# Accumulator banks of their own for each MLP stage, attention steps skewed over three chunks, and a reordered start, in a fused retention and MLP kernel

## The chip, the cores and the metric

The kernel runs on one core of one Trainium2 chip. The metric is the device time of one execution in microseconds (us). The kernel before and the changed one were measured in the same rounds. Two levels occur, about 2 us apart in the kernel before, and where a difference is that small, runs of the same granted TensorE clock (the share of its full rate that TensorE was given, as a mean over the run) are compared.

## The reference

Eight batches of eight heads, 576 positions, head size 64. The scores of q and k are scaled by 1/8 and multiplied by a decay that is lower triangular, `gamma_h ** (i - j)`; there is no softmax. The result (4608 tokens by 512) goes through an MLP with the activation `h * cos(h)`.

```python
scores = scale * np.matmul(q, k.transpose(0, 1, 3, 2))
ret = scores * np.where(rel >= 0, gamma ** rel, 0.0)
attn = np.matmul(ret, v)                      # then (b, h, s, d) -> x[b*s, h*d]
h = x @ w_in                                  # 4608 x 512 @ 512 x 2048
out = (h * np.cos(h)) @ w_out                 # 2048 -> 512
```

## The kernel before

Attention works on chunks of at most 128 positions of one batch (five per batch, the last of 64; 40 in all). The decay is split into a factor in k's position, folded into v by GpSimd (`wv`), and one in q's position, applied at the end (`up`), so earlier chunks enter through a 64 by 64 state per head (`st`). A chunk passes through these steps:

- cast of q, k, v to bf16 (`nat`);
- T: eight transposes into the bank `tp`, one copy by ScalarE to `qk`;
- S: score matmuls into `sc`, masked by VectorE into `pt`;
- ST: the state into `st`, masked by VectorE into `sbd`;
- O: the outputs into `tp` again, scaled by VectorE into `xt`.

The MLP works on blocks of 512 tokens. A first-stage unit is four matmuls of 512 columns into a bank `ml`; ScalarE takes the sine of it shifted by a quarter turn (`cb`), VectorE multiplies (`gt`). A second-stage tile is 16 matmuls of 512 columns in four units; ScalarE evicts it (`os`) and it is stored. The program divides PSUM, the memory that matmuls write to, into eight banks of 512 columns: one `tp`, two `sc`, one `st`, and four `ml`, over which both stages rotate together.

Each engine takes its instructions in the order in which the program adds them (in the profile of this kernel ScalarE's copy for chunk 0, whose transposes end at 7.9 us, starts at 16.66, behind the cast of chunk 3's q, which waits for its load until 16.12); a helper adds the semaphore waits that the named buffers require.

```python
def bank(self):                       # both MLP stages
    i = self.n_ml % 4
    self.n_ml += 1
    return i, self.ML[i]
...
def mlp1(self, j, f):
    i, ps = self.bank()               # four matmuls, sine, product
...
def mlp2(self, j, t, qd):
    if qd == 0:
        self.m2 = self.bank()         # one bank for four units
...
def steps(g):
    def prep():
        cast_to(g + 3)
        load_to(g + 3 + self.NSTG - 1)
        self.step_t(g)
    yield prep
    yield lambda: self.step_s(g)
    if CHUNKS[g][1] < 4:
        yield lambda: self.step_st(g)
    yield lambda: self.step_o(g)

load_to(4)
cast_to(4, ("act", "dve", "pool"))    # q on ScalarE, k on VectorE, v on GpSimd
for s in range(4):
    self.load_win(s)                  # 512 KB slabs of weights, GpSimd's queue
for s in range(4):
    self.load_wout(s)
load_to(self.NSTG)
done = need[0]
for g in range(done):                 # chunks 0 to 3, one after another
    for st in steps(g):
        st()
for j in range(-1, NTB):              # then, for each block: first stage of j+1,
    ...                               # second stage of j, and the steps of the
                                      # chunks of j+2 spread between the units
```

Of the kernel before, what the change touches and what calls it, by code (L numbers as in the profile page):

```python
# [101 lines left out]
class Kernel:  # L102
# [78 lines left out]
    def load_chunk(self, g):  # L181
        b, r, n = CHUNKS[g]
        slot = g % self.NSTG
        for i in (1, 0, 2):
            self.P.add("sp", lambda e, i=i: e.dma_start(  # L185
                ap(self.STG[slot], 3 * DM, 0, n, i * DM, [D, H], [1, D]),
                bass.AP(self.src[i], (b * H * S + CH * r) * D, [[D, n], [S * D, H], [1, D]])),
                w=[("stg", slot, i)], sem=f"i{slot}_{i}")

    def load_win(self, s):  # L190
        self.P.add("pool", lambda e: e.dma_start(
            ap(self.WIN, 4 * DFF, 0, 128, s * 512, [DFF, 4], [1, 512]),
            bass.AP(self.w_in, s * 512, [[DFF, 128], [128 * DFF, 4], [1, 512]])),
            w=[("win", s)], sem=f"wi{s}")

    def load_wout(self, s):
        self.P.add("pool", lambda e: e.dma_start(
            ap(self.WOUT, NF * DM, 0, 128, s * 4 * DM, [DM, 4], [1, DM]),
            bass.AP(self.w_out, s * 4 * 128 * DM, [[DM, 128], [128 * DM, 4], [1, DM]])),
            w=[("wout", s)], sem=f"wo{s}")  # L200
# [19 lines left out]
    def step_t(self, g):  # L220
        b, r, n = CHUNKS[g]
        na, qk = self.NAT[g % self.NNAT], self.QK[g % self.NQK]
        tb = self.T.ap().bitcast(BF16)

        def mm(e, i):
            for c in range(4):
                inst = e.transpose(  # L227
                    tb[:, (1 - i) * 512 + c * 128:(1 - i) * 512 + c * 128 + n],
                    ap(na, 3 * DM, 0, n, i * DM + 128 * c, [1, 128]),
                    ap(self.IDN, 128, 0, n, 0, [1, n]))  # L230
            return inst

        for i in (1, 0):
            self.P.add("pe", lambda e, i=i: mm(e, i), r=[("nat", g % self.NNAT, i), "idn"], w=["tp"])
        w = [("qk", g % self.NQK)]
        self.P.add("act", lambda e: e.activation(  # L236
            ap(qk, 1024, 0, 128, 0, [128, 8], [1, n]),
            tb.rearrange("p (c n) -> p c n", c=8)[:, :, 0:n], AF.Copy), r=["tp"], w=w)

    def step_s(self, g):  # L240
        b, r, n = CHUNKS[g]
        qk, pt = self.QK[g % self.NQK], self.PT[g % self.NPT]

        def mm(e):
            for c in range(4):
                for hp in range(2):
                    inst = e.matmul(  # L247
                        ap(self.SC, 1024, 0, n, hp * 512 + c * 128, [1, n]),
                        ap(qk, 1024, 64 * hp, 64, c * 128, [1, n]),
                        ap(qk, 1024, 64 * hp, 64, 512 + c * 128, [1, n]),  # L250
                        start=True, stop=True, skip_group_check=True)
            return inst

        self.P.add("pe", mm, r=[("qk", g % self.NQK)], w=["sc"])
        self.P.add("dve", lambda e: e.tensor_tensor(  # L255
            ap(pt, 1024, 0, n, 0, [128, 8], [1, n]),
            ap(self.SC, 1024, 0, n, 0, [128, 8], [1, n]),
            ap(self.TRI, 128, 0, n, 0, [0, 8], [1, n]), ALU.mult),
            r=["sc", "tri"], w=[("pt", g % self.NPT)])
# [22 lines left out]
    def step_o(self, g):  # L282
        b, r, n = CHUNKS[g]
        na, qk, pt = self.NAT[g % self.NNAT], self.QK[g % self.NQK], self.PT[g % self.NPT]
        sbd = self.SBD[(g - 1) % self.NSB]

        def inter(e):
            for c in range(4):
                inst = e.matmul(  # L289
                    ap(self.T, 512, 0, 128, c * 128, [1, n]),  # L290
                    ap(sbd, 512, 0, 128, c * 128, [1, 128]),
                    ap(qk, 1024, 0, 128, 512 + c * 128, [1, n]),
                    start=(c == 0), stop=True, skip_group_check=True)
            return inst

        def intra(e):
            for c in range(4):
                for hp in range(2):
                    inst = e.matmul(  # L299
                        ap(self.T, 512, 64 * hp, 64, c * 128, [1, n]),  # L300
                        ap(na, 3 * DM, 0, n, 2 * DM + (2 * c + hp) * D, [1, D]),
                        ap(pt, 1024, 0, n, hp * 512 + c * 128, [1, n]),
                        start=(r == 0 and c == 0), stop=True, skip_group_check=True)
            return inst

        if r:
            self.P.add("pe", inter, r=[("sbd", (g - 1) % self.NSB), ("qk", g % self.NQK)], w=["tp"])
        self.P.add("pe", intra, r=[("nat", g % self.NNAT, 2), ("pt", g % self.NPT)], w=["tp"])
        self.P.add("dve", lambda e: e.tensor_tensor(  # L309
            ap(self.XT, 4 * TOK, 0, 128, b * S + CH * r, [TOK, 4], [1, n]),  # L310
            ap(self.T, 512, 0, 128, 0, [128, 4], [1, n]),
            ap(self.UP, 4 * S, 0, 128, CH * r, [S, 4], [1, n]), ALU.mult),
            r=["tp", "up"], w=[("xt", g)])


    def bank(self):
        i = self.n_ml % 4
        self.n_ml += 1
        return i, self.ML[i]

    def mlp1(self, j, f):
        i, ps = self.bank()
# [3 lines left out]
        xts = [("xt", g) for g, (b, r, n) in enumerate(CHUNKS)  # L326
               if b * S + CH * r < TB * (j + 1) and b * S + CH * r + n > TB * j]

        def mm(e):
            for c in range(4):  # L330
                inst = e.matmul(  # L331
                    ps.ap(), ap(self.WIN, 4 * DFF, 0, 128, c * DFF + 128 * f, [1, 128]),
                    ap(self.XT, 4 * TOK, 0, 128, c * TOK + TB * j, [1, TB]),
# [4 lines left out]
        self.P.add("act", lambda e: e.activation(cb.ap(), ps.ap(), AF.Sin, bias=self.CPI.ap(), scale=1.0),  # L338
                   r=[("ml", i), "cpi"], w=[("cb", ci)])
        self.P.add("dve", lambda e: e.tensor_tensor(  # L340
            ap(gt, NF * TB, 0, 128, f * TB, [1, TB]), ps.ap(), cb.ap(), ALU.mult),
            r=[("ml", i), ("cb", ci)], w=[("gt", j % 2, f)])

    def mlp2(self, j, t, qd):
        if qd == 0:
            self.m2 = self.bank()
        i, ps = self.m2
        gt = self.GT[j % 2]

        def mm(e, f):  # L350
            return e.matmul(  # L351
                ps.ap(), ap(gt, NF * TB, 0, 128, f * TB + 128 * t, [1, 128]),
                ap(self.WOUT, NF * DM, 0, 128, f * DM, [1, DM]),
                start=(f == 0), stop=(f == NF - 1))

        for f in range(4 * qd, 4 * qd + 4):
            self.P.add("pe", lambda e, f=f: mm(e, f), r=[("gt", j % 2, f), ("wout", f // 4)], w=[("ml", i)])
        if qd == 3:
            o = self.n_os % self.NOS
            self.n_os += 1  # L360
            self.P.add("act", lambda e: e.activation(self.OS[o].ap(), ps.ap(), AF.Copy),  # L361
                       r=[("ml", i)], w=[("os", o)])
            self.P.add("sp", lambda e: e.dma_start(
                bass.AP(self.out, (TB * j + 128 * t) * DM, [[DM, 128], [1, DM]]), self.OS[o].ap()),
                r=[("os", o)], sem=f"o{o}")


    def schedule(self):
        need = []
        for j in range(NTB):  # L370
            need.append(1 + max(g for g, (b, r, n) in enumerate(CHUNKS) if b * S + CH * r < TB * (j + 1)))
        state = {"loaded": 0, "cast": 0}

        def load_to(g):
            while state["loaded"] < min(g, len(CHUNKS)):
                self.load_chunk(state["loaded"])
                state["loaded"] += 1

        def cast_to(g, engs=("pool", "pool", "pool")):
            while state["cast"] < min(g, len(CHUNKS)):  # L380
# [3 lines left out]
        def steps(g):  # L384
            def prep():
                cast_to(g + 3)
                load_to(g + 3 + self.NSTG - 1)
                self.step_t(g)
            yield prep
            yield lambda: self.step_s(g)  # L390
            if CHUNKS[g][1] < 4:
                yield lambda: self.step_st(g)
            yield lambda: self.step_o(g)

        load_to(4)
        cast_to(4, ("act", "dve", "pool"))
        for s in range(4):
            self.load_win(s)
        for s in range(4):
            self.load_wout(s)  # L400
        load_to(self.NSTG)
        done = need[0]
        for g in range(done):
            for st in steps(g):
                st()
        for j in range(-1, NTB):
            todo = []
            if j + 2 < NTB:
                for g in range(done, need[j + 2]):
                    todo += list(steps(g))  # L410
                done = need[j + 2]
            n, k = len(todo), 0
            for i in range(16):
                if j + 1 < NTB:
                    self.mlp1(j + 1, i)
                while k < n * (2 * i + 1) / 32:
                    todo[k]()
                    k += 1
                if j >= 0:
                    self.mlp2(j, i // 4, i % 4)  # L420
                while k < n * (2 * i + 2) / 32:
                    todo[k]()
                    k += 1
# [38 lines left out]
```

## Time and profile before

| kernel before | |
|---|---|
| time, median | 390.75 us (390.64 to 392.42, 4 runs) |
| span of the profiled run | 389.2 us |
| TensorE busy | 84% |
| VectorE, ScalarE busy | 48%, 42% |
| first MLP matmul recorded | 38.0 us |
| part with block 1's second stage begins | 110.3 us |
| last block (second stage only) begins | 372.3 us |

A row of the timeline shows the start, the duration, the engine, the source line, the operation with what it writes and reads, the shape, the number of instructions, and in brackets the idle time before it and what ended that. The first extract is TensorE in the kernel before: two chunks of the head, and one tile end of the part without attention. L227 is T, L247 is S, L267 is ST, L289 and L299 are O, L331 the first stage, L351 the second.

```profile
17.72 0.61 PE L247 MATMUL sc<-qk 64*128 64x128 bf16 x8 [9.80 <-ACT qk L236]
18.26 0.61 PE L267 MATMUL st<-nat 128*128 128x128 bf16 x4
19.65 0.64 PE L299 MATMUL tp<-pt,nat 128*64 128x128 bf16 x8 [0.78 <-DVE pt L255]
21.08 1.03 PE L227 MATMUL tp<-idn,nat 128*128 128x128 bf16 x8 [0.79 <-DVE xt L309]
23.23 0.61 PE L247 MATMUL sc<-qk 64*128 64x128 bf16 x8 [1.12 <-ACT qk L236]
...
38.02 1.48 PE L331 MATMUL ml<-xt,win 128*128 128x512 bf16 x3 [1.20 <-DVE xt L309]
...
346.37 1.03 PE L331 MATMUL ml<-xt,win 128*128 128x512 bf16 x4
347.23 1.03 PE L351 MATMUL ml<-wout,gt 128*128 128x512 bf16 x4
348.95 1.04 PE L331 MATMUL ml<-xt,win 128*128 128x512 bf16 x4 [0.69 <-ACT os L361]
```

In the head, one score group follows the other after 5.5 us (17.72, 23.23), and TensorE is busy for about half of that (2.8 us). At 347.23 the last unit of a tile starts. Units follow each other every 0.86 us, so the next could start at 348.09; it starts at 348.95. The duration of a matmul is modelled to its end in the pipe (379 ns for 512 columns), while the next can start 216 ns after it; so every idle time on TensorE is shown about 0.16 us too short.

The second extract is the view of waits of TensorE (in total, number, longest):

```profile
PE sc L247 <- ACT qk L236: 16.7, 14, 9.8
PE ml L331 <- ACT os L361: 15.3, 25, 0.9
PE tp L227 <- DVE xt L309: 6.5, 7, 2.0
```

The first and third belong mostly to the start (14.8 and 5.9 us of them lie before 72 us). The second is spread over the whole kernel: a first-stage unit takes the bank that a finished tile has just left and waits for ScalarE's eviction.

### The profile page before, as it was taken

Reading aid. Unit: us, or ns where it says so; the run is one execution under the profiler, and the core shown is the slowest. Engines: PE = TensorE matmul, PEld = TensorE weight load, DVE = VectorE, ACT = ScalarE, POOL = GpSimd, SP = SyncE. Lnnn points to the kernel's source line nnn. Section 1 sums busy time; section 2 is a strip of 40 time slices with the busy share of each in tenths; the row PEclk is TensorE's granted clock in tenths of the full one; section 3 lists DMA queues with packets and bytes.
Section 4 is the critical chain, followed back from the end, with each engine's and each line's share of the span. In section 5 each row is a group of like instructions: output and inputs, shape, how many; then the busy total and the mean of one; then the engine's idle time right before and its main releaser. Section 6 shows DMA issues by size and latency. Waiting matters only on the chain.

```text
span 389.2 us, 5828 instructions
## 1 busy us (share of the span) xinstructions
PE 326.4 (84%) x2325; PEld 160.0 (41%) x2368; DVE 185.4 (48%) x283; ACT 162.3 (42%) x231; POOL 91.3 (23%) x128
## 2 busy tenths in 40 slices
PE   1156877889988999989889999998999899989996
PEld 0033433344444444444444444444444444434442
DVE  2245466645554555545554655455555555433310
ACT  6222445344443544445435444444444444444421
POOL 2390147522223222312222222321331000000000
PEclk9999989999999999999999999999999999999999
DMA  9999999995448254552675245442000000010012
GB/s 177 201 201 196 196 214 215 204 216 129 108 116 183 69 109 108 115 103 69 142 155 109 69 108 109 108 109 67 31 27 29 27 29 29 27 48 33 29 54 81
DMA packets 121946, 42.31 MB, mean 109 GB/s; under 512 B 113216, under 2 KB 117312, under 8 KB 121920
## 3 DMA queue, kind: packets, MB, share of 16 engines
q1 hardware_dynamic: 117696, 37.76, 45.9%
q0 software_dynamic: 4224, 4.19, 6.3%
q8 instruction: 18, 0.29, 0.3%
q14 instruction: 8, 0.07, 0.1%
HBM read 36.70 MB, written 9.44 MB: 119 GB/s over the span
## 4 chain that ended last, share of the span: by engine, by line
PE 73%; ACT 12%; DVE 7%; issue 3%; SPq 3%; DMA 1%; DVEq 0%; ACTq 0%
PE ml L331 31%; PE ml L351 30%; ACT qk L236 5%; ACT os L361 4%; PE tp L227 4%; PE sc L247 3%; ACT cb L338 3%; DVE gt L340 3%; PE tp L299 3%; SPq L185 3%; DVE pt L255 2%; DVE xt L309 2%; PE st L267 1%; DMA stg<-in_q_dram 1%; PE tp L289 1%
## 5 line engine op out<-in xcount | busy, mean ns | idle before, releaser
L340 DVE TENSOR_TENSOR gt<-ml,cb 128x512 bf16<-128x512 f32 x144 | 99.5, 691 | 160.3 <-ACT cb L338 142.1
L338 ACT ACTIVATE cb<-ml,cpi 128x512 bf16<-128x512 f32 x144 | 98.9, 687 | 168.8 <-PE ml L331 168.8
L331 PE MATMUL ml<-xt,win 128*128 128x512 bf16 x549 | 147.4, 387 | 24.9 <-ACT os L361 15.3
L351 PE MATMUL ml<-wout,gt 128*128 128x512 bf16 x560 | 143.4, 380 | 2.2 <-issue 0.9
L331 PEld LDWEIGHTS ml<-xt,win 128*128 128x128 bf16 x576 | 50.4, 99 | 84.0 <-ACT os L361 22.9
L351 PEld LDWEIGHTS ml<-wout,gt 128*128 128x128 bf16 x576 | 52.2, 98 | 57.2 <-ACT os L361 1.2
L212 POOL CAST nat<-stg 128x512 bf16<-128x512 f32 (+1 forms) x72 | 42.5, 613 | 140.6 <-PE st L267 117.1
L214 POOL TENSOR_TENSOR nat<-stg,wv 128x512 bf16<-128x512 f32 (+1 forms) x40 | 41.7, 1043 | 61.8 <-PE tp L299 38.6
L255 DVE TENSOR_TENSOR pt<-sc,tri 128x1024 bf16<-128x1024 f32 (+1 forms) x40 | 44.3, 1109 | 13.8 <-PE sc L247 13.7
L236 ACT ACTIVATE qk<-tp 128x1024 bf16<-128x1024 bf16 (+1 forms) x40 | 37.3, 933 | 24.1 <-PE tp L227 24.1
L227 PE MATMUL tp<-idn,nat 128*128 128x128 bf16 (+1 forms) x320 | 25.3, 226 | 13.2 <-DVE xt L309 6.5
L227 PEld LDWEIGHTS tp<-idn,nat 128*128 128x128 bf16 (+1 forms) x320 | 19.9, 103 | 26.4 <-DVE xt L309 10.8
L361 ACT ACTIVATE os<-ml 128x512 f32<-128x512 f32 x36 | 21.5, 597 | 22.2 <-PE ml L351 22.0
L247 PE MATMUL sc<-qk 64*128 64x128 bf16 (+1 forms) x320 | 16.4, 226 | 16.7 <-ACT qk L236 16.7
L309 DVE TENSOR_TENSOR xt<-tp,up 128x512 bf16<-128x512 f32 (+1 forms) x40 | 25.2, 631 | 0.6
L247 PEld LDWEIGHTS sc<-qk 64*128 64x128 bf16 (+1 forms) x320 | 9.5, 102 | 33.8 <-ACT qk L236 26.1
L276 DVE TENSOR_TENSOR sbd<-st,bdm 128x512 bf16<-128x512 f32 x32 | 21.8, 681 | 0.0
L299 PE MATMUL tp<-pt,nat 128*64 128x128 bf16 (+1 forms) x320 | 16.7, 230 | 2.9 <-DVE pt L255 2.9
L299 PEld LDWEIGHTS tp<-pt,nat 128*64 128x64 bf16 (+1 forms) x320 | 10.3, 114 | 9.9 <-DVE pt L255 4.8
L267 PE MATMUL st<-nat 128*128 128x128 bf16 x128 | 13.3, 230 | 0.0
L289 PEld LDWEIGHTS tp<-qk,sbd 128*128 128x128 bf16 x128 | 10.0, 104 | 7.2 <-issue 0.5
L267 PEld LDWEIGHTS st<-nat 128*128 128x128 bf16 x128 | 9.9, 102 | 7.3 <-issue 0.6
(26 smaller groups left out, 32.6 us busy)
## 6 DMA issues: line engine op xcount, KB each, us to landing
out_dram<-os SPq DMA_DIRECT2D x36, 256.0 KB, 2.1
stg<-in_k_dram SPq DMA_DIRECT2D x32, 256.0 KB, 4.6
stg<-in_q_dram SPq DMA_DIRECT2D x32, 256.0 KB, 4.7
stg<-in_v_dram SPq DMA_DIRECT2D x32, 256.0 KB, 4.7
win<-in_moe_w_in_dram POOLq DMA_DIRECT2D x4, 512.0 KB, 10.9
wout<-in_moe_w_out_dram POOLq DMA_DIRECT2D x4, 512.0 KB, 22.3
stg<-in_k_dram SPq DMA_DIRECT2D x8, 128.0 KB, 3.4
stg<-in_q_dram SPq DMA_DIRECT2D x8, 128.0 KB, 3.8
```

The source lines that it names most:

```text
L212: fn = lambda e, dst=dst, src=src: e.tensor_copy(dst, src)
L214: self.P.add(engs[2], lambda e: e.tensor_tensor(ap(nat, 3 * DM, 0, n, 2 * DM, [D, H], [1, D]), ap(stg, 3 * DM, 0, n, 2 * DM, [D, H], [1, D ...
L227: inst = e.transpose(tb[:, (1 - i) * 512 + c * 128:(1 - i) * 512 + c * 128 + n], ap(na, 3 * DM, 0, n, i * DM + 128 * c, [1, 128]), ap(self ...
L236: self.P.add("act", lambda e: e.activation(ap(qk, 1024, 0, 128, 0, [128, 8], [1, n]), tb.rearrange("p (c n) -> p c n", c=8)[:, :, 0:n], AF ...
L247: inst = e.matmul(ap(self.SC, 1024, 0, n, hp * 512 + c * 128, [1, n]), ap(qk, 1024, 64 * hp, 64, c * 128, [1, n]), ap(qk, 1024, 64 * hp, 6 ...
L255: self.P.add("dve", lambda e: e.tensor_tensor(ap(pt, 1024, 0, n, 0, [128, 8], [1, n]), ap(self.SC, 1024, 0, n, 0, [128, 8], [1, n]), ap(se ...
L299: inst = e.matmul(ap(self.T, 512, 64 * hp, 64, c * 128, [1, n]), ap(na, 3 * DM, 0, n, 2 * DM + (2 * c + hp) * D, [1, D]), ap(pt, 1024, 0, ...
L331: inst = e.matmul(ps.ap(), ap(self.WIN, 4 * DFF, 0, 128, c * DFF + 128 * f, [1, 128]), ap(self.XT, 4 * TOK, 0, 128, c * TOK + TB * j, [1, ...
L338: self.P.add("act", lambda e: e.activation(cb.ap(), ps.ap(), AF.Sin, bias=self.CPI.ap(), scale=1.0), r=[("ml", i), "cpi"], w=[("cb", ci)])
L340: self.P.add("dve", lambda e: e.tensor_tensor(ap(gt, NF * TB, 0, 128, f * TB, [1, TB]), ps.ap(), cb.ap(), ALU.mult), r=[("ml", i), ("cb", ...
L351: return e.matmul(ps.ap(), ap(gt, NF * TB, 0, 128, f * TB + 128 * t, [1, 128]), ap(self.WOUT, NF * DM, 0, 128, f * DM, [1, DM]), start=(f ...
L361: self.P.add("act", lambda e: e.activation(self.OS[o].ap(), ps.ap(), AF.Copy), r=[("ml", i)], w=[("os", o)])
```

## The change

It intends three things: (1) from block 1 on the second stage gets bank 3 for itself and the first stage rotates over the other three; only in the last block do the tiles of the second stage rotate over banks (block 0's four tiles run side by side, one in each bank); (2) attention steps are skewed (T of chunk g+2, S of g+1, O of g), so that no step waits for the one just before it; (3) the start is reordered: chunks 0 to 3 are skewed too, using idle MLP banks and sharing the copy between ScalarE and VectorE; block 0 runs its whole MLP slab by slab of weights, block 1's first stage is cut at 192 columns, and loads are gated so that early slabs come first. The last tile is also cut in two column halves.

```diff
 def mlp1(...):
-        i, ps = self.bank()
+        i = self.n_ml % 3
+        self.n_ml += 1
 def mlp2(...):
-        if qd == 0:
-            self.m2 = self.bank()
+        ps = self.ML[bank]            # bank is 3, but rotates in the last block
...
+        def att_to(g0, g1):
+            out = []
+            for g in range(g0, g1):
+                out += [lambda g=g: T(g + 2), lambda g=g: S_(g + 1), lambda g=g: O(g)]
+                if CHUNKS[g][1] < 4:
+                    out.append(lambda g=g: ST(g))
+            return out
...
+        load_to(4)
+        cast_to(3, three)
+        self.load_win(0, [("stg", 3, 1)])      # waits until chunk 3's k has landed
+        self.load_win(1)
+        cast_to(4, three)
+        self.load_win(2)
+        self.load_win(3)
+        self.load_wout(0)
+        self.load_wout(1)
+        load_to(6, [("wout", 0)])
+        def t0(g):
+            self.step_t(g, g % 2)              # q's transposes in bank ml0 or ml1
+        t0(0), self.step_st(0), S_(0)
+        for g in (1, 2, 3):
+            t0(g), O(g - 1, 3), self.step_st(g), S_(g)     # outputs in bank ml3
+        self.mlp1(0, 256, 0)
+        O(3, 3)
+        for f in (1, 2, 3):
+            self.mlp1(0, 256, f)
+        for f in range(4):
+            self.mlp1(256, 512, f)
+        for f in range(4, 16):
+            self.mlp1(0, 512, f)
+        ... # wout 2 and 3, chunks 6 to 8, gated
+        banks = [3, 0, 1, 2]
+        for qd in (0, 1):
+            for t in range(4):
+                self.mlp2(0, t, range(4 * qd, 4 * qd + 4), banks[t])
+        self.step_t(4), S_(4), self.step_t(5), O(4), S_(5), self.step_st(5)
+        ... # the other half of block 0's second stage, with O(5) between
+        ... # block 1's first stage in columns 512:704 and 704:1024,
+        ... # chunks 6 to 13 between
+        for j in range(1, NTB):
+            ... # as before, but att_to(...) between the units
+                mlp.append(m2(j, i // 4, i % 4, (3 + i // 4) % 4 if last else 3))
+            if last:                            # last tile in two column halves
+                mlp = mlp[:12]
+                mlp += [lambda: self.mlp2(j, 3, range(NF), 2, (0, 256)), lambda: self.mlp2(j, 3, range(NF), 3, (256, 512))]
```

## The prediction

> **What bounds the kernel now.** TensorE, once fed. In the timeline from 341 to 372 us (no attention) groups of four 512-column matmuls start 0.863 us apart: 0.216 us each[...]. 1152 of them are 249 us, which the change keeps. From 72.8 to 341.2 us, seven stages of 27.6 us and 24.4 us of TensorE idle (view of waits) leave 50.5 us for 31 attention chunks: about 1.77 us for a full one, 1.15 for a half.
>
> Not bound by TensorE:
> 1. Head. The first MLP matmul starts at 38.0 us. Chunk 0's score matmuls wait until 17.7, because ScalarE's copy stands behind the cast of chunk 3's q (landed 16.1); chunks 0 to 3 then take 5.5 us each (copy 1.02, mask 1.22, scaling 0.69, each waited for).
> 2. Until 72.8 us the first block's 16 first-stage units take 34.8 us, not 13.8 plus attention: weights and chunks share the DMA (chunk 6's v lands at 46 us), and attention waits on its single bank.
> 3. Later, the bank of a finished second-stage tile is next taken by the first stage: 0.69 us idle each time from 341 to 372 us, 15.3 us over the span, waiting for ScalarE's 0.60 us eviction.
>
> **What the change does.**
> - Head: the start at 17.7 stays, since all casts still precede the first copy. Skewing, the split copy and more banks make VectorE the limit: [...]1.22, 0.68, 0.69: about 3.3 us per chunk. MLP runs from about 30.4: 7.5 us gained.
> - Block 0 runs without attention between: first stage to about 46 us[...], half its second stage to 53, chunks 4 and 5 with 2 us of exposed copies to 57, the rest to 65.
> - Block 1's first stage is cut at 192 and 320 columns with four chunks in each part. VectorE has 13 us of work in the first (16 products at about 0.33, plus 7.7) and 17.5 in the second, over TensorE's 11 and 16. I put 15 and 18.5: the interleaved part starts near 99 us. Chunks from 9 on are issued after block 0's outputs, at about 66 us; at 3.8 us each they arrive just in time.
> - Then 193.5 + about 42 for 25 chunks, to 334.5; last block 13.8, to 348.
> - The second stage has bank 3 alone; its eviction hides behind one first-stage unit (0.86). Almost all of the 15 us goes; where a 1.02 us copy precedes the eviction, tenths remain. I allow 6 us for all such waits.
> - End: last eviction and store about 3 us, as now.
>
> Span about 356, time about 357 us (it is 1.6 above the span now): 8.6% less. Range 348 to 368. Faster by over 2%: 0.97; within 2%: 0.025; slower: 0.005.
>
> **What would show it.** First MLP group before 34 us; waits of first-stage matmuls for the eviction below 4 us; VectorE at 80% or score matmuls waiting for copies between 65 and 99 us; interleaved part starting at 95 to 103 us; DMA not full at 50 to 60 us.
>
> **What would make it wrong.** Evictions late behind copies at most tiles (over 10 us); three first-stage banks too few where these units run alone (matmul to product about 2.6 us, three units 2.59); gated weight loads late, so that block 0 waits for a slab; chunks after 8 late, costing 5 to 10 us near 70 to 90 us.

In "Head", the sum of about 3.3 us per chunk contains a term for VectorE's half of the copy that is cut; the three terms left come to 2.59. In "Block 0", 13.8 us of first stage from 30.4 on end at 44.2; what the forecast's "about 46" holds above that was an allowance. The 0.33 us for a product of 192 columns is close to what the traces show: VectorE's scaling takes 0.42 us for 256 columns and 0.69 for 512 in the kernel before, and this product 0.35 in the changed one. The 3.8 us per chunk agree with the 204 to 205 GB/s that the kernel before moved from 40 to 60 us: 768 KB come to 3.8 us.

## The result, and the profile after

| | before | after |
|---|---|---|
| time, median | 390.75 us | 355.03 us (354.27 to 355.91, 4 runs) |
| ratio | | 0.908, 95% interval 0.904 to 0.912 |
| span | 389.2 | 352.5 |
| TensorE busy | 84% | 90% |
| first MLP matmul recorded | 38.0 | 26.5 |
| part with block 1's second stage begins | 110.3 | 96.6 |
| last block begins | 372.3 | 336.1 |

A ratio is the mean time of one kernel's fast runs over that of the other's fast runs of the same rounds, so it is not quite the ratio of the medians.

The table divides the gain in the span (36.7 us): about 13.7 us are won up to the part with block 1's second stage, about 22.5 us between there and the last block, 0.5 us at the end. TensorE in the changed kernel; L229 is now T, L256 is S, L276 ST, L299 and L309 O, L339 the first stage, L358 the second, L371 the eviction:

```profile
17.20 0.61 PE L256 MATMUL sc<-qk 64*128 64x128 bf16 x8 [8.86 <-ACT qk L242]
...
20.24 0.61 PE L256 MATMUL sc<-qk 64*128 64x128 bf16 x8
...
23.40 0.61 PE L256 MATMUL sc<-qk 64*128 64x128 bf16 x8
...
26.12 0.40 PE L256 MATMUL sc<-qk 64*128 64x128 bf16 x8
26.45 0.61 PE L339 MATMUL ml<-xt,win 128*128 128x256 bf16 x4
26.90 0.39 PE L299 MATMUL ml<-qk,sbd 128*128 128x128 bf16 x4
28.38 0.41 PE L309 MATMUL ml<-pt,nat 128*64 128x128 bf16 x8 [1.09 <-DVE pt L264]
28.72 1.48 PE L339 MATMUL ml<-xt,win 128*128 128x256 bf16 x12
...
327.45 1.03 PE L358 MATMUL ml<-wout,gt 128*128 128x512 bf16 x4
328.31 1.03 PE L339 MATMUL ml<-xt,win 128*128 128x512 bf16 x4
329.18 1.03 PE L358 MATMUL ml<-wout,gt 128*128 128x512 bf16 x4
```

Score groups now follow each other after 3.1 us, but the first is still at 17.2. VectorE shows what a chunk now waits for (L264 is the mask, L245 its half of the copy, L319 the scaling, L285 the mask of the state):

```profile
21.02 1.22 DVE L264 TENSOR_TENSOR pt<-sc,tri 128x1024 bf16<-128x1024 f32 x1
22.15 0.41 DVE L245 COPY qk<-ml 128x512 bf16<-128x512 bf16 x1
22.97 0.69 DVE L319 TENSOR_TENSOR xt<-ml,up 128x512 bf16<-128x512 f32 x1 [0.40 <-PE ml L309]
23.58 0.68 DVE L285 TENSOR_TENSOR sbd<-st,bdm 128x512 bf16<-128x512 f32 x1
```

VectorE is idle for only 0.40 us per chunk, while the scaling waits for the output matmuls, which can start only when the mask is done. The copy fits into that time. TensorE is hardly idle either (9.4 of 10 us busy from 17 to 27), because it runs at half its clock here: eight score matmuls take 0.61 us at 23.40 and 0.40 us at 26.12, and in the kernel before the same group took 0.61 us at 54.60, where the clock record says 0.50. The clock record in the trace begins with full clock at 25.4 us, and the views count what lies before it as 1.00. In the kernel before it begins only at 45.2 us, so there the first 7 us of the MLP ran at half clock as well (four 512-column matmuls took 1.68 us, from 41.13 to 42.81, against 0.86 later).

The last three rows on TensorE are a tile end: no bracket. ScalarE in the same stretch of the changed kernel:

```profile
327.65 0.69 ACT L346 ACTIVATE cb<-ml,cpi 128x512 bf16<-128x512 f32 x1 [1.04 <-PE ml L339]
328.51 0.60 ACT L371 ACTIVATE os<-ml 128x512 f32<-128x512 f32 x1 [0.17 <-PE ml L358]
329.38 0.69 ACT L346 ACTIVATE cb<-ml,cpi 128x512 bf16<-128x512 f32 x1 [0.27 <-PE ml L339]
```

The eviction ends at 329.11, and the next tile starts in the same bank at 329.18. One first-stage unit (328.31 to 329.18) covers the eviction, with 0.07 us to spare. The kernel before rotated over four banks and lost 0.86 us at a tile end all the same; what counted was whose turn came next.

The waits of TensorE in the changed kernel, in answer to those of before:

```profile
PE sc L256 <- ACT qk L242: 8.9, 1, 8.9
...
PE tp L299 <- ACT qk L237: 2.9, 4, 1.1
PE ml L339 <- DVE xt L319: 2.4, 4, 0.9
...
PE tp L299 <- DVE pt L264: 2.2, 3, 0.9
PE sc L256 <- ACT qk L237: 1.5, 2, 0.8
...
PE ml L339 <- ACT os L371: 0.7, 1, 0.7
PE ml L358 <- ACT os L371: 0.7, 1, 0.7
```

The eviction costs two waits instead of 26 (25 of the first stage and one of the second). What is left lies in the start: the first row is the wait for chunk 0's copy, and most of the waits of O and S for copy and mask fall between 50 and 97 us.

### The profile page after: what moved, and what is told of

It reads as the page before. It is cut to its first block, busy times and chain, and to the rows that moved or that the text cites. A ratio compares the mean times of both kernels' runs of the same rounds, so it can differ in the third digit from the quotient of the medians.

```text
span 352.5 us, 6098 instructions
## 1 busy us (share of the span) xinstructions
PE 318.1 (90%) x2428; PEld 166.9 (47%) x2464; DVE 189.0 (54%) x307; ACT 165.7 (47%) x252; POOL 90.7 (26%) x128
## 4 chain that ended last, share of the span: by engine, by line
PE 82%; DVE 6%; ACT 5%; SPq 3%; issue 2%; DMA 1%; DVEq 0%
PE ml L358 35%; PE ml L339 34%; PE tp L229 4%; PE sc L256 3%; PE tp L309 3%; SPq L185 3%; ACT cb L346 2%; DVE gt L349 2%; DVE pt L264 2%; ACT qk L237 2%; PE tp L299 2%; PE st L276 2%; DMA stg<-in_q_dram 1%; DVE xt L319 1%; PE ml L309 1%
## 5 line engine op out<-in xcount | busy, mean ns | idle before, releaser
L349 DVE TENSOR_TENSOR gt<-ml,cb 128x512 bf16<-128x512 f32 (+3 forms) x164 | 102.4, 625 | 120.9 <-ACT cb L346 96.4
L346 ACT ACTIVATE cb<-ml,cpi 128x512 bf16<-128x512 f32 (+3 forms) x164 | 103.8, 635 | 125.9 <-PE ml L339 125.6
L339 PE MATMUL ml<-xt,win 128*128 128x512 bf16 (+3 forms) x632 | 145.4, 353 | 5.8 <-DVE xt L319 2.4
L358 PE MATMUL ml<-wout,gt 128*128 128x512 bf16 (+1 forms) x580 | 142.1, 374 | 1.7 <-ACT os L371 0.7
L339 PEld LDWEIGHTS ml<-xt,win 128*128 128x128 bf16 x656 | 57.2, 98 | 57.8 <-DVE xt L319 3.1
L358 PEld LDWEIGHTS ml<-wout,gt 128*128 128x128 bf16 x592 | 53.9, 98 | 59.0 <-ACT os L371 3.1
L214 POOL TENSOR_TENSOR nat<-stg,wv 128x512 bf16<-128x512 f32 (+1 forms) x40 | 41.7, 1043 | 38.1 <-DMA stg<-in_v_dram 16.4
L264 DVE TENSOR_TENSOR pt<-sc,tri 128x1024 bf16<-128x1024 f32 (+1 forms) x40 | 44.3, 1107 | 8.9 <-PE sc L256 8.9
L237 ACT ACTIVATE qk<-tp 128x1024 bf16<-128x1024 bf16 (+1 forms) x36 | 33.3, 926 | 13.4 <-PE tp L229 13.3
L371 ACT ACTIVATE os<-ml 128x512 f32<-128x512 f32 (+1 forms) x37 | 21.7, 586 | 29.9 <-PE ml L358 29.6
L229 PE MATMUL tp<-idn,nat 128*128 128x128 bf16 (+1 forms) x304 | 22.7, 218 | 4.5 <-DVE nat L212 4.5
L256 PE MATMUL sc<-qk 64*128 64x128 bf16 (+1 forms) x320 | 15.8, 221 | 10.3 <-ACT qk L242 8.9
L319 DVE TENSOR_TENSOR xt<-tp,up 128x512 bf16<-128x512 f32 (+1 forms) x36 | 22.5, 624 | 4.0 <-PE tp L309 3.8
L229 PEld LDWEIGHTS tp<-idn,nat 128*128 128x128 bf16 (+1 forms) x304 | 18.4, 99 | 12.9 <-DVE nat L212 4.5
L285 DVE TENSOR_TENSOR sbd<-st,bdm 128x512 bf16<-128x512 f32 x32 | 21.8, 680 | 0.0
L256 PEld LDWEIGHTS sc<-qk 64*128 64x128 bf16 (+1 forms) x320 | 9.2, 99 | 24.1 <-issue 13.0
L299 PE MATMUL tp<-qk,sbd 128*128 128x128 bf16 (+1 forms) x116 | 10.4, 212 | 5.1 <-ACT qk L237 2.9
L309 PE MATMUL tp<-pt,nat 128*64 128x128 bf16 (+1 forms) x288 | 14.1, 219 | 0.8 <-ACT qk L237 0.7
L299 PEld LDWEIGHTS tp<-qk,sbd 128*128 128x128 bf16 x116 | 8.0, 97 | 12.0 <-DVE pt L264 3.0
L276 PE MATMUL st<-nat 128*128 128x128 bf16 x128 | 13.1, 228 | 0.0
L276 PEld LDWEIGHTS st<-nat 128*128 128x128 bf16 x128 | 9.9, 101 | 5.7 <-issue 0.3
## 6 DMA issues: line engine op xcount, KB each, us to landing
wout<-in_moe_w_out_dram POOLq DMA_DIRECT2D x4, 512.0 KB, 11.5
```

The costliest lines, as they stand in the source:

```text
L214: self.P.add(engs[2], lambda e: e.tensor_tensor(ap(nat, 3 * DM, 0, n, 2 * DM, [D, H], [1, D]), ap(stg, 3 * DM, 0, n, 2 * DM, [D, H], [1, D ...
L229: inst = e.transpose(dst[:, c * 128:c * 128 + n], ap(na, 3 * DM, 0, n, i * DM + 128 * c, [1, 128]), ap(self.IDN, 128, 0, n, 0, [1, n]))
L237: self.P.add("act", lambda e: e.activation(ap(qk, 1024, 0, 128, 0, [128, 8], [1, n]), tk.rearrange("p (c n) -> p c n", c=8)[:, :, 0:n], AF ...
L256: inst = e.matmul(ap(self.SC, 1024, 0, n, hp * 512 + c * 128, [1, n]), ap(qk, 1024, 64 * hp, 64, c * 128, [1, n]), ap(qk, 1024, 64 * hp, 6 ...
L264: self.P.add("dve", lambda e: e.tensor_tensor(ap(pt, 1024, 0, n, 0, [128, 8], [1, n]), ap(self.SC, 1024, 0, n, 0, [128, 8], [1, n]), ap(se ...
L276: inst = e.matmul(ap(self.ST, 512, 0, 128, c * 128, [1, 128]), ap(na, 3 * DM, 0, n, DM + c * 128, [1, 128]), ap(na, 3 * DM, 0, n, 2 * DM + ...
```

## The experiments

Theory 1 says that the separate banks carry most of the gain after 100 us. Rival 2 says that the skew does, and that banks alone would only move the wait. For the start, the question is whether the skewed chunks, the first block's order or the gates count. All twelve kernels gave correct results. They were run at other times.

| run | edit | median us | ratio to before |
|---|---|---|---|
| b_banks | before + separate banks | 372.67 | 0.953 |
| b_skew | before + skew beside the blocks | 390.07 | 0.995 |
| b_both | before + both | 368.35 | 0.941 |
| a_shared | after, banks shared again from block 1 on | 372.53 | 0.952 |
| a_tail | after, last block in bank 3 alone | 358.30 | 0.915 |
| a_serial | after, chunks 0 to 3 one after another | 365.13 | 0.935 |
| a_nogates | after, loads not gated | 356.04 | 0.910 |
| a_casts | after, casts in order of arrival | 351.69 | 0.900 |
| a_casts2 | the same, next cast before the mask | 350.64 | 0.893 |
| a_obank | after, outputs of chunks 6 to 12 in bank 3 | 352.56 | 0.902 |
| a_early | after, chunks 4 and 5 spread out | 352.29 | 0.898 |
| a_best | after, all improvements | 342.82 | 0.873 |

### b_banks: the banks alone

```diff
-        i = self.n_ml % 4
+        i = self.n_ml % 3
...
-            self.m2 = self.bank()
+            self.m2 = (3, self.ML[3])
```

> The kernel before, with bank 3 for the second stage alone and three banks rotating for the first stage; nothing else. Theory 1 (separate banks hide the eviction behind one first-stage unit, and this is most of the gain after 100 us): first-stage matmuls wait under 3 us for the eviction instead of 15.3; each of some 25 waits costs 0.69 us of idle plus about 0.16 that lies under the modelled end of the matmul before, so about 20 us: time 367 to 375 us. Rival 2 (the wait only changes place; without the skewed attention the eviction comes late behind copies): second-stage matmuls wait over 8 us for the eviction, time 382 to 391 us.

Measured: 372.67 us, 18.2 us less than before. The first stage no longer waits for the eviction at all; the second waits four times, 3.0 us together (view of waits of this run):

```profile
PE ml L351 <- ACT os L361: 3.0, 4, 0.9
```

Theory 1 holds and the rival falls: half of the whole gain is this two-line edit. The four waits are in the last block, where no first-stage unit stands between two tiles. The 18.2 us are therefore a balance: in the profiles the last block starts 20.9 us earlier than before (351.4 instead of 372.3) and takes 2.6 us longer.

### b_skew: the skew alone

```diff
-                for g in range(done, need[j + 2]):
-                    todo += list(steps(g))
+                    todo += att_to(done, need[j + 2])     # from block 1's first stage on,
+                                                          # started by T, S of the first and T of the next
```

> The kernel before, with the attention steps beside blocks 0 to 8 skewed over three chunks (transposes of chunk g+2, scores of g+1, outputs of g), banks shared as before. Theory 1: the waits of attention after 72.8 us were small (1.9 us for the copy, 0.8 for mask and scaling), so the gain is 1 to 6 us: time 385 to 390 us, waits of first-stage matmuls for the eviction 12 us or more. Rival 2 (skewing removes the loss): time below 380 us.

Measured: 390.07 us, ratio 0.995 with an interval of 0.990 to 1.000: a small gain, 0.8 us in medians and 1.9 us between runs of equal clock (388.8 against 390.8 at 0.995, 390.9 against 392.9 at 0.991; means; by span it is 2.5 and 3.1). Its waits show where the skew's gain went:

```profile
PE ml L331 <- ACT os L361: 17.4, 28, 0.9
```

The wait for the eviction grew from 15.3 us (25 times) to 17.4 us (28 times). The likely reason, read from the counts and not tested, is that some waits of attention had fallen between a tile's end and the next use of its bank, and there had hidden an eviction.

### b_both: banks and skew together

The two edits above in one kernel, with the start as before.

> The kernel before with both: separate banks and skewed attention; head, order of loads and first block as before. Theory 1: the two add up, and what is left against the changed kernel is the first 110 us alone, some 12 to 14 us: time 366 to 371 us; from the start of block 1's second stage to the last block's end 238 to 242 us, as in the changed kernel (239.4), against 261.7 before. Rival 2: the first block's order is also worth something later (time above 374 us).

Measured: 368.35 us, 4.3 us below the banks alone in medians. The two kernels met the two levels in different shares; at equal clock it is 5.5 us (0.995) and 4.7 us (0.991), where the skew by itself had given 1.9. With the bank free, the waits of attention are the last ones left, and the skew removes them: from 110 to 345 us the attention and MLP matmuls waited 6.3 us with banks alone and 2.8 us here. From the part with block 1's second stage to the start of the last block this run takes 238.0 us (107.6 to 345.5; weight loads of the traces), as expected; the expectation says "end", but its 239.4 and 261.7 are measured to that start. What remains against the changed kernel is 13.3 us, as expected, but the expectation put it all in the first 110 us. The trace says otherwise. Here is this run's last block:

```profile
345.55 3.63 PE L351 MATMUL ml<-wout,gt 128*128 128x512 bf16 x16 [0.69 <-ACT os L361]
349.86 3.63 PE L351 MATMUL ml<-wout,gt 128*128 128x512 bf16 x16 [0.69 <-ACT os L361]
...
```

Tiles follow each other after 4.32 us, where 16 matmuls take 3.45. From the start of the last block to the end this run takes 19.6 us, the changed kernel 16.4. So about 3 us of the 13.3 lie at the end.

### a_shared: the changed kernel without its banks

```diff
-        i = self.n_ml % 3
+        i = self.n_ml % (4 if lo >= 2 * TB else 3)
...
+        if j >= 1 and bank is None:       # second stage takes the next of the four
+            if fs[0] == 0:
+                self.m2 = self.n_ml % 4
+                self.n_ml += 1
+            bank = self.m2
```

> The changed kernel, but with both stages rotating over all four banks from block 1 on, as before. Theory 1: 28 tile ends wait 0.69 to 0.86 us each again: time 371 to 379 us, first-stage matmuls wait 13 to 20 us for the eviction; up to 97 us the trace is the same. Rival 2 (the skew did it): below 362 us.

Measured: 372.53 us, 17.5 us more than the changed kernel (17.4 at equal clock). The brackets of 0.69 us are back at tile ends and the first stage waits 12.9 us for the eviction (expected: 13 to 20). The last block rotates in both of these kernels, so this compares with the 20.9 us of b_banks: up to the last block the banks are worth some 17 to 21 us.

### a_tail: the last block in bank 3 alone

```diff
-                mlp.append(m2(j, i // 4, i % 4, (3 + i // 4) % 4 if last else 3))
+                mlp.append(m2(j, i // 4, i % 4, 3))
-            if last:
-                mlp = mlp[:12]
-                mlp += [...]              # two column halves
```

> The changed kernel with its last block as the bank rule alone would have it: all four tiles in bank 3, none cut in halves. Theory: with no first-stage unit between, each of the three further tiles waits 0.69 us idle (0.86 us in starts) for the eviction, and the last eviction and store are those of a whole tile: 2.5 to 3.5 us more, 357 to 358 us at granted clock 1.00; it closes the sum of the parts (banks 18, skew beside them 6, head 9.5, end 3). Rival (the end is hidden by the stores that follow): below 355.5 us at the same clock.

Measured: 357.48 and 357.72 us in the runs at clock 1.00, against 354.27 and 354.29 of the changed kernel at that clock: 3.3 us, as expected. In the profiles the last block takes 19.6 us instead of 16.5: three starts lost by 0.86 us make 2.6 of it, and the two column halves the other 0.5 (the kernel before rotates without halves and takes 17.0). Rotation in the last block is a part of its own, and needed once the banks are separate.

### a_serial: chunks 0 to 3 one after another

```diff
-        t0(0), self.step_st(0), S_(0)
-        for g in (1, 2, 3):
-            t0(g), O(g - 1, 3), self.step_st(g), S_(g)
+        for g in range(4):
+            self.step_t(g), S_(g), self.step_st(g), O(g)
         self.mlp1(0, 256, 0)
-        O(3, 3)
```

> The changed kernel, but chunks 0 to 3 done one after another as before (transposes and outputs in the one attention bank, one copy on ScalarE, outputs before the next chunk's transposes). Theory: the head's gain is this skew and nothing else; chunks take 5.5 us instead of 3.1 again, the first MLP group starts at 36 to 38 us instead of 26.5, and the time rises by 7 to 10 us: 362 to 365. Rival (the first block's order is what was gained; it would catch up later because its slabs of weights arrive in time either way): below 358 us.

Measured: 365.13 us, 10.1 us more; the first MLP group starts at 36.7 us and nothing is caught up. The skew of the first four chunks, with the split copy and the spare banks that belong to it, is thus worth 10 us (9.8 and 10.3 at equal clock), and together with the end (3.3) it makes up the 13.3 us that b_both lacks. Within about 1 us nothing is left over for the order of the first block. The view of windows shows why; its columns are the stretch, its length, the busy times of TensorE, its weight loads, VectorE, ScalarE and GpSimd, the granted clock, the share of DMA (the whole time of the packets that start in the stretch, so it can exceed 1) and GB/s. First b_both, which keeps the old order:

```profile
36.00:56.00 20.00, 15.25 (x113) 7.54 (x117) 9.45 (x16) 7.13 (x10) 5.16 (x7) 0.91 1.17 203
56.00:76.00 20.00, 15.27 (x139) 7.66 (x139) 14.08 (x20) 9.19 (x13) 12.82 (x17) 1.00 1.21 209
76.00:96.00 20.00, 19.84 (x151) 10.13 (x153) 10.83 (x15) 11.24 (x16) 3.82 (x5) 1.00 1.12 226
96.00:110.00 14.00, 13.68 (x105) 6.99 (x105) 8.39 (x13) 6.78 (x11) 4.35 (x6) 1.00 0.40 90
```

and a_serial, which has the new one:

```profile
36.00:56.00 20.00, 19.28 (x103) 9.00 (x104) 13.00 (x23) 11.96 (x20) 11.16 (x16) 1.00 1.12 206
56.00:76.00 20.00, 16.72 (x150) 9.25 (x149) 5.21 (x9) 6.56 (x12) 1.46 (x2) 1.00 0.22 69
76.00:96.00 20.00, 16.40 (x216) 11.65 (x213) 16.08 (x33) 12.43 (x24) 13.41 (x19) 1.00 1.13 215
96.00:110.00 14.00, 12.68 (x137) 8.01 (x136) 11.40 (x19) 9.20 (x15) 6.55 (x9) 1.00 1.17 213
```

Both have the first MLP group near 37 us. The new order fills TensorE from 36 to 56 us (19.3 against 15.3 us busy) and leaves it emptier from 76 to 110 (29.1 against 33.5); over the 74 us the sums are 65.1 and 64.0. The idle time was moved, because the attention that was put off must be done later in a stretch with short units. The traces give the same balance in starts: from the first weight load of the MLP to the start of the last block it is 307.9 us in b_both, one fall of the clock included (0.91 from 36 to 56 us), and 308.8 us here.

### a_nogates: loads without gates

```diff
-        self.load_win(0, [("stg", 3, 1)])
+        self.load_win(0)
...
+        self.load_wout(2)
+        self.load_wout(3)
-        load_to(6, [("wout", 0)])
+        load_to(7)
```

> The changed kernel without the gates on loads: all eight weight loads issued at once after the casts of chunk 3, chunks 4 to 6 at once, 7 and 8 as slots come free. Theory: in the kernel before, win had landed by about 37 us and wout by 50, so TensorE meets at most short waits for a slab: 354 to 358 us, waits of TensorE for weights under 2 us. Rival (the gates keep the slabs ahead of TensorE): waits for win of 4 us or more between 27 and 45 us, time above 359.

Measured: 356.04 us (354.40 to 356.23; the changed kernel 354.27 to 355.91). At equal clock the two agree within 0.3 us (354.40 against 354.27 and 354.29 at 1.00). No wait for weights appears. The gates are worth nothing measurable here.

### a_casts: casts in order of arrival

The first scores wait until 17.2 us because ScalarE has the casts of all four chunks in front of chunk 0's copy. Here each cast stands just before its chunk's transposes.

```diff
-        cast_to(3, three)
-        self.load_win(0, [("stg", 3, 1)])
-        self.load_win(1)
-        cast_to(4, three)
+        cast_to(1, three)
...
         for g in (1, 2, 3):
+            cast_to(g + 1, three)
+            ... # for g == 2 the two loads of win taken out above
             t0(g), O(g - 1, 3), self.step_st(g), S_(g)
```

> The changed kernel with the casts of chunks 1 to 3 placed in order of arrival, each just before its own transposes, so that ScalarE's copy of chunk 0 no longer stands behind the cast of chunk 3. Theory: first scores near 8 to 9 us instead of 17.2, the four chunks then follow the DMA at 3.6 us each, MLP starts at 19 to 21 us, and the gain is 5 to 8 us: 347 to 350. Rival (the slabs of weights, issued from 15 us on, become the bound): MLP waits for win, gain below 3 us: 352 or more.

Measured: 351.69 us, a gain of 3.3 us (2.7 at clock 1.00): less than theory, and no wait for weights either, so neither was right. The first scores do start at 8.5 us, but TensorE then waits for VectorE's cast of the next k before each T (5.9 us in three waits). VectorE in this run:

```profile
14.32 1.22 DVE L264 TENSOR_TENSOR pt<-sc,tri 128x1024 bf16<-128x1024 f32 x1
15.45 0.42 DVE L212 CAST nat<-stg 128x512 bf16<-128x512 f32 x1
...
19.21 1.22 DVE L264 TENSOR_TENSOR pt<-sc,tri 128x1024 bf16<-128x1024 f32 x1
```

The edit put the cast behind the mask of the chunk before; chunks follow after 4.9 us. One wait in a queue had been exchanged for another. One cast on VectorE also took 1.09 us instead of 0.42: it began at 10.32 us, 0.23 us after a product of 1.04 us on GpSimd, and ended 0.28 us after it. The cause was not tested.

### a_casts2: the next cast before the mask

```diff
-        t0(0), self.step_st(0), S_(0)
+        t0(0), self.step_st(0), cast_to(2, three), S_(0)
         for g in (1, 2, 3):
-            t0(g), O(g - 1, 3), self.step_st(g), S_(g)
+            t0(g), O(g - 1, 3), self.step_st(g)
+            cast_to(min(g + 2, 4), three)
+            ... # for g == 1 the first two loads of win
+            S_(g)
```

> As the run that placed the casts in order of arrival, but the cast of the next chunk's k stands before the mask on VectorE instead of behind it, so that the next transposes don't wait for the mask. Theory (what was missing there was this one place in VectorE's queue: 4.9 us per chunk instead of 3.6): chunks 2 and 3 follow at 3.2 to 3.7 us, the first MLP group starts at 19.5 to 21.5 us instead of 23.9, time 346.5 to 349.5. Rival (the slabs of weights now bound it): first MLP group waits for win, time 351 or more.

Measured: 350.64 us (349.50 to 351.58), outside the expectation of 346.5 to 349.5 except for one run. The head did what theory said, and the rival holds as well: chunks follow after 3.6 us and the first MLP group starts at 21.1 us, now waiting for its weights.

```profile
21.11 0.61 PE L339 MATMUL ml<-xt,win 128*128 128x256 bf16 x4 [0.96 <-DMA win<-in_moe_w_in_dram]
...
48.99 0.61 PE L276 MATMUL st<-nat 128*128 128x128 bf16 x4 [0.92 <-POOL nat L214]
49.82 5.65 PE L358 MATMUL ml<-wout,gt 128*128 128x512 bf16 x15 [0.22 <-issue]
```

5.3 us were won by 21 us. Part of them is given back near 50 us: chunk 5's v comes late, and after the idle time around chunks 4 and 5 the 16 matmuls (15 are recorded) that should take 3.6 us take 5.65, most of them at half clock (the granted clock was 0.50 from 48 to 52 us). The run without that fall took 349.50 us, the one with most of it 351.58 (mean clock 1.00 and 0.99).

### a_obank: outputs of chunks 6 to 12 in the free bank

While block 1's first stage runs alone (62 to 97 us), bank 3 is idle and T and O share one bank.

```diff
-        att = [..., lambda: T(7), lambda: O(6), ...]
+        att = [..., lambda: T(7), lambda: O(6, 3), ...]     # the same for chunks 7 to 12
```

> The changed kernel with the outputs of chunks 6 to 12 written to bank 3, which is free while block 1's first stage runs alone, so that they no longer wait for the copy of the next chunk's transposes out of the shared attention bank. Theory (VectorE bounds this part, 90% busy at 70 to 80 us): waits move from the copy to the mask, gain 0 to 1.5 us: 353.5 to 355.5. Rival (the shared bank bounds it): waits for the copy between 62 and 97 us fall from 4.4 to under 1.5 us and the time to 352 or less.

Measured: 352.56 us; at clock 1.00 351.76 and 351.81, so 2.5 us less than the changed kernel. That is beyond the expectation of theory and just what the rival expected. From 62 us on the waits for the copy fall to 0.8 us (the changed kernel has 3.3 there; the 4.4 of the expectation is not what its trace shows), and waits of O for the mask of 2.6 us stay (2.2). So the shared bank cost 2.5 us; VectorE, still 93% busy from 70 to 80 us, is not the whole limit.

### a_early: chunks 4 and 5 spread out

```diff
-        for qd in (0, 1):
-            for t in range(4):
-                self.mlp2(0, t, range(4 * qd, 4 * qd + 4), banks[t])
-        self.step_t(4), S_(4), self.step_t(5), O(4), S_(5), self.step_st(5)
+        for t in range(4):
+            self.mlp2(0, t, range(4), banks[t])
+        self.step_t(4)
+        self.mlp2(0, 0, range(4, 8), banks[0])
+        S_(4), self.step_t(5)
+        for t in (1, 2):
+            self.mlp2(0, t, range(4, 8), banks[t])
+        O(4), S_(5)
+        self.mlp2(0, 3, range(4, 8), banks[3])
```

with ST and O of chunk 5 after the third quarter.

> The changed kernel, with the steps of chunks 4 and 5 placed between the first quarters of block 0's second stage, instead of all together after the second quarter. Theory: the 1.8 us of exposed copies near 51 to 54 us go, and with them the idle time after which, in some runs, the granted clock falls to half for some 3 us (seen in the profile of the run with outputs in bank 3: clock 0.50 at 54 to 56 us): median 352 to 353.6, all runs within 0.7 us of each other, clock 0.998 or more in each. Rival (the two levels 1.5 us apart have another cause): the levels stay, spread 1.3 us or more.

Measured: 352.29 us, all runs within 0.25 us of each other (352.16 to 352.41), mean clock 0.999 or 1.000 in each. The two levels are gone, and the 1.8 us of idle time as well. Their cause shows in the profile of a_obank, which had caught the slower level (view of windows, columns as above; the seventh figure after the stretch, ahead of the DMA share, is the clock):

```profile
50.00:52.00 2.00, 1.31 (x21) 0.69 (x20) 0.00 (x0) 0.60 (x1) 1.37 (x3) 1.00 1.24 223
52.00:54.00 2.00, 0.88 (x20) 0.66 (x19) 0.68 (x1) 1.02 (x1) 1.33 (x2) 1.00 1.27 211
54.00:56.00 2.00, 2.00 (x23) 1.19 (x20) 1.66 (x3) 0.00 (x0) 1.38 (x3) 0.50 0.77 135
56.00:58.00 2.00, 2.00 (x8) 0.76 (x7) 0.59 (x1) 0.00 (x0) 1.10 (x2) 0.64 0.00 0
```

After 4 us in which TensorE was busy for 2.2, the clock falls to 0.50 for some 3.4 us. The two levels of the changed kernel, 354.27 and 354.29 us at a mean clock of 1.00 and 355.77 and 355.91 at 0.995, put its cost at about 1.5 us. In the profiled run of the kernel before the clock record has such a fall too: 0.50 for 3.4 us from 52.0 us on, after 2 us (50 to 52) in which TensorE was busy for 0.04. The profiled run of the changed kernel had the same idle time at the same place (2.2 us busy from 50 to 54) and no fall. What decides whether the clock falls after such idle time is not shown by these runs. One fall of 3.4 us makes a mean clock of 0.995 or 0.996 over a run, and two make 0.990 or 0.991.

### a_best: all improvements together

The edits of a_casts2, a_obank and a_early, and two changes of banks so that no tile starts in a bank just finished:

```diff
-        banks = [3, 0, 1, 2]
+        banks = [2, 0, 1, 3]
...
-                ... (3 + i // 4) % 4 if last else 3
+                ... (2 + i // 4) % 3 if last else 3
```

> All together: casts in order of arrival with the next k before the mask, chunks 4 and 5 between block 0's first quarters, outputs of chunks 6 to 12 in bank 3, and the order of banks at both ends of the kernel such that no tile starts in the bank just finished (0.69 us at 62 and at 335 us). Theory: the gains add up, 7 + 2 + 2.5 + 1.4 us: 341 to 345. Rival (chunks 9 and later, issued after block 0's outputs, or the gated weights become the bound): 347 or more.

Measured: 342.82 us, ratio 0.873 to before, against 0.908 of the changed kernel: the gains add up. TensorE is 94% busy in a span of 339.5 us. With chunks 4 and 5 spread out, the head's gain is no longer given back. The runs again show two groups (twice 341.22, four times 342.80 to 343.10), and here the mean clock is 1.00 in all. That does not show that the clock was the same, since the mean leaves out the half clock of the start, before the first record (in the one run with a trace, which is of the faster group, eight score matmuls still take 0.61 us at 19.21). No trace of the slower group was kept, so the cause is open.

## Why the prediction was right

The prediction was 357 us, in a range of 348 to 368; 355.03 was measured. The steps:

- **Head.** Predicted: start at 17.7 unchanged, 3.3 us per chunk, MLP from 30.4, 7.5 us gained. Measured: 17.2, 3.1 us, 28.7 (the first group at 26.5), 10.1 us by a_serial. The mechanism was right: VectorE was the limit but for 0.4 us per chunk, in which the scaling waited for outputs. Two things were missed: the copy took 0.41 us, where the sum of 3.3 leaves 0.7 for it, and fit into that wait, and TensorE ran at half clock until 25.4 us. The start came 0.5 us earlier, and the four chunks took 11.5 us instead of 12.7; what a_serial shows beyond these 1.7 us is not taken apart.
- **Blocks 0 and 1.** Predicted against measured: first stage of block 0 done at 46 and 43.3, half its second stage 53 and 50.4, chunks 4 and 5 done 57 and 54.8, block 1's parts 15 and 18.5 us long against 14.9 and 18.9, interleaved part from 99 and 96.6. Most of the 2 to 3 us of difference is the earlier start. The allowance in block 0's 46 us was not needed; the granted clock was 1.00 from 25.4 us on. The stated reason for the two parts, VectorE, was only partly right: a_obank shows that the shared attention bank cost 2.5 us of them.
- **Eviction.** Predicted: 15 us of waits, almost all of it gone. Shown: the waits of the first stage for it fell from 25 to one, but the worth up to the last block was 20.9 us in b_banks (18.2 with the loss in the last block), where 15.3 us shown and 0.16 us hidden in each of 25 waits would be 19.4. The total did not suffer, since the prediction added up TensorE's work and waits anew instead of subtracting 15 from the old time. The hidden part must sit in its price per chunk of 1.77 us, which was derived with the same view: of the 239.4 us measured, 193.5 of MLP and 4.9 of waits leave 41.0 for the 25 chunks, against about 42.
- **Skew beside the blocks.** It got no number of its own; 6 us were allowed for waits of all kinds, and 4.9 us were left from 99 to 337 us. Most of its 4.3 us (4.7 to 5.5 at equal clock) exist only once the banks are separate; alone it gave 1.9.
- **End.** Predicted: 13.8 us for the last block and about 3 us after it, "as now". Measured: 16.5 us for both (17.0 before). What the prediction doesn't say is that this holds only because the last block rotates its banks; by the rule of the other blocks, and without the halves, it would have been 3.3 us worse (a_tail).
- **What would make it wrong.** None of the four came: tile ends meet no late evictions, three banks cost three waits of 0.2 us in all, no slab was late, and chunks from 9 on were issued at 63 us (66 predicted) and came in time.

The parts, measured one by one in medians, are 18.2 (banks), 4.3 (skew with them), 10.1 (skew of the first four chunks) and 3.3 us (end): 35.9 of 35.7. The first two were added to the kernel before and the last two taken from the changed one, and medians mix the two levels, so that the sum closes to 0.2 us is partly luck; 1 us is what it can show. Within that, gates and the order of the first block contribute nothing on top. That the order's gain was eaten by short units later is read from the windows and not tested by itself.

## What to carry to other kernels

When two stages with different lifetimes rotate over one pool of accumulator banks, look at who gets the bank that was just finished: here a bank reserved for the long-lived accumulator was enough, because one unit of the other stage (0.86 us) lasted until the eviction (0.60 us) had ended, 0.07 us to spare; where no such unit stands between, rotate (3.3 us in a_tail). Add such waits up from starts, not from the idle times shown for pipelined matmuls (0.69 us shown for 0.86 lost), and expect that removing a smaller wait shows little until the larger one that follows is gone (1.9 us for the skew alone, 4.7 to 5.5 with the banks). A cast or copy placed too early in an in-order queue holds up everything behind it (the first scores at 17.2 us, and at 8.5 in a_casts), so place each just ahead of its use, and look again at what it now stands behind.
